# Output copies of a block at the end of one slot, and x split on VectorE in one place

## The chip, the cores and the metric

The kernel runs on one core of a Trainium2 chip. The metric is the device time of one execution in microseconds, as the median of several runs; less is better. Five engines work beside each other: TensorE (PE; its weight loads are shown apart as PEld), VectorE (DVE), ScalarE (ACT), GpSimd (POOL) and SyncE (SP), whose queue issues the kernel's DMAs. Each engine runs its own instructions strictly in the order of the program, and waits for the others through semaphores.

## The reference

Attention inside chunks of 64 tokens, then two feed-forward layers, all in fp32 from the reader's point of view:

```python
# q, k, v: 8 batches, 8 heads, 576 tokens, 64 wide; chunks of 64
scores = scale * q_c @ k_c.T ; scores -= max ; attn = exp(scores)
attn = attn / (attn.sum(-1) + 1e-9) ; x = (attn @ v_c) laid out as (4608 tokens, 512)
h = x @ w_in                                   # 512 -> 2048
g = where(h > 0, h, exp(min(h, 0)) - 1)        # ELU
y = g @ w_out                                  # 2048 -> 512
out = (sigmoid(y @ w_gate) * (y @ w_val)) @ w_out2   # 512 -> 1536 -> 512
```

## The kernel before

**Numbers.** Every product of a feed-forward layer is made of three fp32r matmuls: each operand is split into a rounded high part and a low part (raw minus high), and high x high, low x high and high x low are summed in PSUM (PASSES). To split a tile takes a cast on one engine and a subtraction on another (split, L94 to L96). The weights come as 64-bit numbers and are converted on the chip: a tile of raw bits is loaded on SP's queue (load, L118) and goes through ScalarE steps (magnitude L124, low L128, high) and five VectorE steps (clamp, shift, sign, add L146, rest L155). add also issues the load of the raw tile that is *ahead* places further on, which takes over the buffer that add has just read. bg(n) puts n such steps into the program.

**Blocks and slots.** The 4608 tokens are 9 blocks of 512 (j = 0 to 8). Phase A goes through each block in 16 slots (f = 0 to 15, s = 16 j + f). slot(s) (L461) writes out by hand what each engine does in a slot; nothing is reordered later. In a slot PE does, in this order: one attention product (scores of a pair of chunks in an even slot, values in an odd one, four matmuls on the PSUM tile banks), the first layer of slot s (layer_1: 12 matmuls into h, three for each of the four x tiles kk = 0 to 3), and the second layer of slot s - 2 (layer_2: 12 matmuls that add into four PSUM banks y0 to y3, one bank for each e). The y banks fill over a block: the last addition for block j - 1 is in slot f = 1 of block j, and in slot f = 2 the first layer_2 of block j overwrites them. Between the two lie the four copies of y_out (L449: e even on ScalarE, L456; e odd on VectorE, L458), each followed by a DMA to ymid on SP (L459).

**The elementwise work of a slot.** ScalarE and VectorE turn h into g: elu_exp (L405) and elu_rest (L408) on ScalarE, elu_sum (L411) on VectorE one slot later, then elu_split (cast on ScalarE, L90; subtraction on VectorE, L96). The attention of a pair runs over four slots: first_parts copies half of banks to s1 on ScalarE (L297), softmax_max (L310 to L312), softmax_exp (L315), softmax_sum, and blocks_out (a VectorE transpose to dt, L339, and eight small DMAs to tt, L346); two slots later transposes_split makes pt from tt (L92 and L96 on VectorE, two casts on ScalarE, L357), which the values product (L379) of the slot after needs as weights. In odd slots VectorE also splits the next pair's operands (L248, L256 to L258) and writes the pair's result into xr (L395).

**The x tiles.** xr0 to xr3 hold the attention result of the next block, xs0 to xs3 its split halves; there is one buffer of each, so xs of the next block can be written only when layer_1 of slot f = 15 has read the old one, and layer_1 of slot f = 0 needs it 16 matmuls later. Before, split_x (L182) is called at four places: x0 in slot 15 ahead of the second half of layer_1 (subtraction on GpSimd), x1 behind elu_split (VectorE), x2 behind elu_rest (GpSimd), x3 at the start of slot f = 0 (VectorE). The cast is always ScalarE's.

**Buffers.** The pool e gives out 3 buffers of 2 KB a partition, in turn to the elu tiles, the y copies, and in phase B to the sigmoid and output tiles. s1, dt and tt have 2 buffers each. Phase B (L685) runs the last block of phase A and then the second network, in slots of 36 matmuls (pg, pv at L189, o at L730), while it converts 36 weight tiles with 4 raw buffers.

Of the kernel before, what the change touches and what calls it, by code (L numbers as in the profile page):

```python
# [8 lines left out]
F32 = mybir.dt.float32  # L9
# [8 lines left out]
CH = 64  # L18
# [5 lines left out]
NB = NT // TB  # L24
NG = NT // 128 * (H // 2)
GPB = NG // NB
KC = DM // 128
# [25 lines left out]
def kernel(  # L53
# [23 lines left out]
    nc = tc.nc  # L77
# [3 lines left out]
    w_p = ctx.enter_context(tc.tile_pool(name="w", bufs=2 * F1))  # L81
    x_p = ctx.enter_context(tc.tile_pool(name="x", bufs=1))
    g_p = ctx.enter_context(tc.tile_pool(name="g", bufs=2))
    e_p = ctx.enter_context(tc.tile_pool(name="e", bufs=3))
    ps_y = ctx.enter_context(tc.tile_pool(name="ps_y", bufs=1, space=bass.MemoryType.PSUM))
    ps_h = ctx.enter_context(tc.tile_pool(name="ps_h", bufs=2, space=bass.MemoryType.PSUM))

# [94 lines left out]
    def split_x(key, kk, lo_eng):  # L182
        x = xs[key, kk] = x_p.tile([128, 2, TB], F32R, tag=f"xs{kk}", name=f"xs{kk}")
        split(xr.pop((key, kk)), x[:, 0], x[:, 1], nc.scalar, lo_eng)
# [18 lines left out]
    def phase_a():  # L203
        with (
# [7 lines left out]
            raws, vals, qv, kz, st = {}, {}, {}, {}, {}  # L212
# [79 lines left out]

            def first_parts(P, what):

                t = st[P, what + "1"] = s_p[0].tile([128, 4, CH], F32, tag="s1", name="s1", bufs=2)
                for a, p in enumerate(halves):
                    nc.scalar.copy(out=t[p], in_=parts_of(st[P, what], p, a)[0])  # L297

# [36 lines left out]

            def blocks_out(P):

                d = s_p[0].tile([128, 2, 4, 32], F32, tag="dt", name="dt", bufs=2)
                nc.vector.transpose(  # L339
                    out=d.rearrange("p b n q -> p n b q"),  # L340
                    in_=st.pop((P, "p")).rearrange("p n (b k) -> p n b k", b=2),
                )
                t = st[P, "tt"] = s_p[0].tile([64, 4, 128], F32, tag="tt", name="tt", bufs=2)
                for b in range(2):
                    for w in range(4):
                        nc.sync.dma_start(  # L346
                            out=t[32 * b:32 * b + 32, w],
                            in_=d[32 * w:32 * w + 32, b].rearrange("p n q -> p (n q)"),
                        )
# [99 lines left out]
            def y_out(j, es=range(KC)):  # L449
                for e in es:  # L450
                    if j == NB - 2:
                        y = xr_tile("y", e)
                    else:
                        y = e_p.tile([128, TB], F32, tag="e", name="y")
                    if e % 2 == 0:
                        nc.scalar.copy(out=y, in_=y_t.pop((j, e)))  # L456
                    else:
                        nc.vector.tensor_copy(out=y, in_=y_t.pop((j, e)))  # L458
                    nc.sync.dma_start(out=ymid[j][:, e], in_=y)  # L459

            def slot(s, steps=0):  # L461


                j, f = divmod(s, F1)
                q = [steps // 4 + (i < steps % 4) for i in range(4)]
                last = f == F1 - 1
                nxt = j + 1 if j + 1 < NB else ("b", 0)
                even = s % 2 == 0
                P, T, V, N = s // 2 + 1, (s + 1) // 2, (s - 1) // 2, (s + 3) // 2

                def is_pair(n, least=0):
                    return least <= n < NP

                if even:
                    if is_pair(P + 1, P32):
                        load_raw(P + 1)
                    if is_pair(P):
                        scores(P)
                    if is_pair(P, P32):
                        first_parts(P, "s")  # L480
                else:
                    if is_pair(V):
                        values(V)
                    if is_pair(V, P32):
                        first_parts(V, "v")
                    elif is_pair(V):
                        values_out(V)
                if f == 0 and j > 0:
                    split_x(j, KC - 1, nc.vector)
                if s >= F1:  # L490
                    elu_sum(s - 1)
                if even and is_pair(P):
                    softmax_max(P)
                if even and is_pair(P, P32):
                    softmax_exp(P)
                if even and is_pair(P - 1, P32):
                    transposes_split(P - 1)
                if even and is_pair(P, P32):
                    softmax_sum(P)
                    blocks_out(P)  # L500
                if not even:
                    if is_pair(N, P32):
                        split_k(N)
                    if is_pair(V, P32):
                        values_out(V)
                    if is_pair(N, P32):
                        split_qkv(N)
                bg(q[0])
                if 0 < s < F1:
                    elu_sum(s - 1)  # L510
                if s >= EARLY:
                    layer_1(s, 2)
                if f == 2 and j > 0:
                    y_out(j - 1, (2, 3))
                if s == F1 - 1:

                    layer_1(s, 3)
                    transposes(T)
                    transposes_out(T)
                if last:  # L520
                    split_x(nxt, 0, nc.gpsimd)
                bg(q[1])
                layer_1(s)
                if s > 0:
                    elu_split(s - 1)
                if even and 0 <= P < P32:
                    softmax_exp(P)
                if last:
                    split_x(nxt, 1, nc.vector)
                now = not even and 0 <= T < P32 and s >= F1  # L530
                if now:
                    transposes(T)
                elu_exp(s)
                if now:
                    transposes_out(T)
                if even and PB <= P < P32:
                    softmax_sum(P)
                bg(q[2])
                if 0 < s <= F1:
                    elu_low(s - 1)  # L540
                elu_rest(s)
                if last:
                    split_x(nxt, 2, nc.gpsimd)
                bg(q[3])
                if even and is_pair(P) and P < PB:
                    softmax_sum(P)
                if s >= 2:
                    layer_2(s - 2)
                if not even and is_pair(T) and s < F1 - 1:
                    transposes(T)  # L550
                    transposes_out(T)
                if f == 1 and j > 0:
                    y_out(j - 1, (0, 1))

            def first_block(load_w):

# [128 lines left out]
    def phase_b(slot, layer_2, elu_sum, elu_split, y_out):  # L685
        with (
# [2 lines left out]
            tc.tile_pool(name="ps_b", bufs=2, space=bass.MemoryType.PSUM) as ps_b,  # L689
        ):  # L690
            tiles = [(k, w_src[k[0]][k[1]], w_p if n < 2 * F1 else w2_p) for n, k in enumerate(w2)]
            load_w = convert(tiles, conv_p, 4, 4)
            for n in range(4):
                load_w(n)
            for s in range((NB - 1) * F1, NB * F1):
                slot(s, A8_STEPS if s < NB * F1 - 1 else 0)
# [157 lines left out]
```

## Time and profile before

| what | value |
|---|---|
| median of 3 runs | 1809.66 us (1807.86 to 1810.4) |
| profiled execution, device time | 1808.78 us |
| its span, first to last instruction | 1807.0 us |
| PE busy | 1776.1 us, 98% |
| VectorE busy | 1044.9 us, 58% |
| ScalarE busy | 757.1 us, 42% |
| GpSimd busy | 44.2 us, 2% |

The profile page gives the busy time of each engine over the whole span, the same in 40 slices, the chain of work that ended last, and groups of instructions by line. The answers of the trace that are used below are the list of waits (who waited for whom, in total), and timelines: every instruction in order of time, with equal neighbours merged (xN), and in brackets the idle time of the engine before it and what ended it. A PE row's length is modelled and overlaps the next row; the distance between the starts of two PE rows is what counts.

### The profile page before, as it was taken

What the parts mean: (1) busy time and instruction counts of PE and PEld (TensorE: products, weight loads), DVE (VectorE), ACT (ScalarE), POOL (GpSimd) and SP (SyncE); (2) the same over time, 40 slices, a digit from 0 to 9 for tenths busy, and PEclk for the clock granted to TensorE, in tenths of its full rate; (3) what the DMA queues carried; (4) which work ended last, traced back from release to release, by engine and by line L of the source; (5) the groups of instructions that cost most, each with busy time, mean ns of one, the idle gap of its engine ahead of it and who ended that gap; (6) DMA issues with size and microseconds to landing.
All of it is one profiled execution on the core that took longest, in us unless ns stands there. A gap on an engine that the chain in (4) does not pass through costs nothing.

```text
span 1807.0 us, 21535 instructions
## 1 busy us (share of the span) xinstructions
PE 1776.1 (98%) x8068; PEld 1471.1 (81%) x8068; DVE 1044.9 (58%) x1980; ACT 757.1 (42%) x1411; POOL 44.2 (2%) x50
## 2 busy tenths in 40 slices
PE   7999999999999999999999999999999999999999
PEld 6887878788888878788888888888888888888887
DVE  7997888888888888887767423222222222222322
ACT  7775666767666766767654201010110101010101
POOL 1000000000000000000000000000000000000000
PEclk9999999999999999999999999999999999999999
DMA  6652121121212122215343101000010101010000
GB/s 231 200 169 77 57 80 59 58 69 53 74 57 82 48 79 59 69 47 166 117 128 106 47 1 47 1 24 24 9 38 0 47 0 48 1 47 1 24 1 24
DMA packets 61593, 111.52 MB, mean 62 GB/s; under 512 B 11056, under 2 KB 30000, under 8 KB 61488
## 3 DMA queue, kind: packets, MB, share of 16 engines
q1 hardware_dynamic: 61488, 110.14, 19.3%
q8 instruction: 63, 1.03, 0.2%
q14 instruction: 42, 0.34, 0.1%
HBM read 84.15 MB, written 18.87 MB: 57 GB/s over the span
## 4 chain that ended last, share of the span: by engine, by line
PE 83%; DVE 9%; ACT 5%; issue 1%; DMA 1%; SPq 0%; POOL 0%; DVEq 0%
PE o L730 16%; PE pv L189 16%; PE pg L189 16%; PE y L441 16%; PE h L189 15%; PE banks L379 1%; PE banks L280 1%; ACT pt L357 1%; DVE t L140 1%; DVE elu L411 1%; DVE s L310 1%; DVE w L155 1%; DVE xs L96 1%; DVE qv L258 1%; DVE t L146 1%
## 5 line engine op out<-in xcount | busy, mean ns | idle before, releaser
L189 PE MATMUL h<-xs,w 128*128 128x512 f32 x1728 | 426.3, 394 | 5.7 <-DVE xs L96 3.9
L441 PE MATMUL y<-g,w 128*128 128x512 f32 x1728 | 419.5, 391 | 8.3 <-ACT y L456 7.6
L719 DVE TENSOR_TENSOR sg<-pv,sg 128x512 f32<-128x512 f32 x108 | 74.6, 691 | 548.6 <-PE pv L189 545.6
L441 PEld LDWEIGHTS y<-g,w 128*128 128x128 f32 x1728 | 323.2, 188 | 80.2 <-ACT y L456 10.1
L189 PEld LDWEIGHTS h<-xs,w 128*128 128x128 f32 x1728 | 317.1, 189 | 69.0 <-DVE xs L96 6.4
L714 ACT ACTIVATE sg<-pg 128x512 f32<-128x512 f32 x108 | 64.5, 597 | 676.9 <-PE pg L189 676.6
L189 PE MATMUL pv<-xs,w 128*128 128x512 f32 x1296 | 311.3, 389 | 0.0
L189 PE MATMUL pg<-xs,w 128*128 128x512 f32 x1296 | 311.3, 389 | 0.0
L730 PE MATMUL o<-w,g 128*128 128x512 f32 x1296 | 311.1, 389 | 0.0
L189 PEld LDWEIGHTS pv<-xs,w 128*128 128x128 f32 x1296 | 243.2, 188 | 50.5
L189 PEld LDWEIGHTS pg<-xs,w 128*128 128x128 f32 x1296 | 243.2, 188 | 50.5
L730 PEld LDWEIGHTS o<-w,g 128*128 128x128 f32 x1296 | 243.2, 188 | 50.5
L411 DVE SCALAR_TENSOR_TENSOR elu<-h,elu 128x512 f32<-128x512 f32 x144 | 99.4, 690 | 65.5 <-ACT elu L408 64.2
L405 ACT ACTIVATE elu<-h 128x512 f32<-128x512 f32 x144 | 86.0, 597 | 53.6 <-PE h L189 25.6
L297 ACT COPY s<-banks 64x256 f32<-64x256 f32 x216 | 78.2, 362 | 67.5 <-PE banks L280 64.3
L90 ACT CAST g<-elu 128x512 fp32r<-128x512 f32 x144 | 89.3, 620 | 23.0 <-DVE elu L411 18.5
L408 ACT ACTIVATE elu<-elu 128x512 f32<-128x512 f32 x144 | 90.9, 631 | 3.8
L96 DVE TENSOR_TENSOR g<-elu,g 128x512 fp32r<-128x512 f32 x128 | 87.9, 686 | 6.3 <-ACT g L90 4.6
L96 DVE TENSOR_TENSOR g<-sg,g 128x512 fp32r<-128x512 f32 x108 | 74.9, 694 | 3.7
L96 POOL TENSOR_TENSOR xs<-xr,xs 128x512 fp32r<-128x512 f32 x26 | 36.8, 1417 | 1631.1 <-ACT xs L90 1631.1
L315 ACT ACTIVATE e<-s 128x256 f32<-128x256 f32 x64 | 26.8, 418 | 111.2 <-DVE s L312 110.7
L357 ACT CAST pt<-pt 64x512 fp32r<-64x512 f32 x108 | 66.8, 619 | 4.5 <-DVE pt L92 2.2
(86 smaller groups left out, 1299.2 us busy)
## 6 DMA issues: line engine op xcount, KB each, us to landing
raw<-in_qkv SPq DMA_DIRECT2D x54, 512.0 KB, 3.7
wraw<-in_w_out SPq DMA_DIRECT2D x28, 512.0 KB, 3.5
xr<-ymid SPq DMA_DIRECT2D x36, 256.0 KB, 3.6
wraw<-in_w_in SPq DMA_DIRECT2D x16, 512.0 KB, 3.7
ymid<-y SPq DMA_DIRECT2D x32, 256.0 KB, 3.1
out<-o SPq DMA_DIRECT2D x32, 256.0 KB, 2.0
tt<-dt SPq DMA_DIRECT2D x432, 16.0 KB, 1.8
wraw<-in_w_gate SPq DMA_DIRECT2D x12, 512.0 KB, 3.6
```

Of the source, the lines that this page charges most:

```text
L90: nc.scalar.copy(out=out, in_=raw)
L96: lo_eng.tensor_sub(out=lo, in0=raw, in1=hi)
L189: nc.tensor.matmul(out=ps, lhsT=w[:, zw, kk * 128:(kk + 1) * 128], rhs=xs[key, kk][:, zx], start=(kk == 0 and n == 0), stop=(kk == KC - 1 ...
L297: nc.scalar.copy(out=t[p], in_=parts_of(st[P, what], p, a)[0])
L357: nc.scalar.copy(out=t[h1, z], in_=t[h0, z])
L405: nc.scalar.activation(out=e_t[s], in_=h_t[s], func=ACTF.Exp)
L408: nc.scalar.activation(out=e_t[s], in_=e_t[s], func=ACTF.Relu, scale=-1.0, bias=1.0)
L411: nc.vector.scalar_tensor_tensor(out=e_t[s], in0=h_t.pop(s), scalar=0.0, in1=e_t[s], op0=ALU.max, op1=ALU.subtract,)
L441: nc.tensor.matmul(out=y_t[j, e], lhsT=w[:, zw, e * 128:(e + 1) * 128], rhs=g[:, zx], start=(f == 0 and n == 0), stop=(f == F1 - 1 and n = ...
L714: nc.scalar.activation(out=sg, in_=pg, func=ACTF.Sigmoid)
L719: nc.vector.tensor_tensor(out=sg, in0=pv, in1=sg, op=ALU.mult)
L730: nc.tensor.matmul(out=o_t[t], lhsT=g[:, zx, t * 128:(t + 1) * 128], rhs=w[:, zw], start=(f == 0 and n == 0), stop=(f == F2 - 1 and n == 2),)
```

## The change

- All four output copies of block j - 1 are called at the end of slot f = 1 of block j. Before, y0 and y1 stood there, and y2 and y3 in slot f = 2 behind the first half of layer_1.
- The four split_x of a block are called in a row in slot f = 15, right behind layer_1 and ahead of elu_split, all with the subtraction on VectorE. For the switch to phase B only three are made there; the fourth stays where it was.
- The pool e has 5 buffers instead of 3. s1, dt and tt have 1 instead of 2, and phase B has 3 raw weight buffers instead of 4.

```diff
-    e_p = ctx.enter_context(tc.tile_pool(name="e", bufs=3))
+    e_p = ctx.enter_context(tc.tile_pool(name="e", bufs=5))
...
-                t = st[P, what + "1"] = s_p[0].tile([128, 4, CH], F32, tag="s1", name="s1", bufs=2)
+                t = st[P, what + "1"] = s_p[0].tile([128, 4, CH], F32, tag="s1", name="s1")
...
-                d = s_p[0].tile([128, 2, 4, 32], F32, tag="dt", name="dt", bufs=2)
+                d = s_p[0].tile([128, 2, 4, 32], F32, tag="dt", name="dt")
...
-                t = st[P, "tt"] = s_p[0].tile([64, 4, 128], F32, tag="tt", name="tt", bufs=2)
+                t = st[P, "tt"] = s_p[0].tile([64, 4, 128], F32, tag="tt", name="tt")
...
-                if f == 0 and j > 0:
-                    split_x(j, KC - 1, nc.vector)
...
-                if f == 2 and j > 0:
-                    y_out(j - 1, (2, 3))
...
-                if last:
-                    split_x(nxt, 0, nc.gpsimd)
                 bg(q[1])
                 layer_1(s)
+                if last:
+                    for kk in range(KC if j + 1 < NB else KC - 1):
+                        split_x(nxt, kk, nc.vector)
                 if s > 0:
                     elu_split(s - 1)
...
-                if last:
-                    split_x(nxt, 1, nc.vector)
...
-                if last:
-                    split_x(nxt, 2, nc.gpsimd)
...
                 if f == 1 and j > 0:
-                    y_out(j - 1, (0, 1))
+                    y_out(j - 1)
...
-            load_w = convert(tiles, conv_p, 4, 4)
-            for n in range(4):
+            load_w = convert(tiles, conv_p, 3, 4)
+            for n in range(3):
                 load_w(n)
```

**VectorE, from slot 15 of block 2 to slot 0 of block 3.** The rows run from the split of q (qv) to the first softmax rows (s) of the next slot; xs_N is a split x tile, made from xr_N; the fp32 subtraction g is elu_split's. Before:

```order
L258 TENSOR_TENSOR qv<-raw,qv 64x2x256
L96 TENSOR_TENSOR g<-elu,g 128x512
L96 TENSOR_TENSOR xs_3403<-xr_2783,xs_3403 128x512
L96 TENSOR_TENSOR xs_3433<-xr_3257,xs_3433 128x512
L411 SCALAR_TENSOR_TENSOR elu<-h,elu 128x512
L310 TENSOR_TENSOR s<-banks,s_3430 64x256 x2
```

And after the change:

```order
L258 TENSOR_TENSOR qv<-raw,qv 64x2x256
L96 TENSOR_TENSOR xs_3397<-xr_2530,xs_3397 128x512
L96 TENSOR_TENSOR xs_3400<-xr_2783,xs_3400 128x512
L96 TENSOR_TENSOR xs_3403<-xr_3020,xs_3403 128x512
L96 TENSOR_TENSOR xs_3406<-xr_3257,xs_3406 128x512
L96 TENSOR_TENSOR g<-elu,g 128x512
L411 SCALAR_TENSOR_TENSOR elu<-h,elu 128x512
L310 TENSOR_TENSOR s<-banks,s_3433 64x256 x2
```

Two subtractions have come over from GpSimd, and all four now stand ahead of the subtraction of g.

**ScalarE, at the same place**, from the casts of q to the first_parts copy (s_N, the name of s1) of slot 0. Before:

```order
L255 CAST qv<-raw 64x2x256
L90 CAST xs_3391<-xr_2530 128x512
L90 CAST g<-elu 128x512
L90 CAST xs_3403<-xr_2783 128x512
L405 ACTIVATE elu<-h 128x512
L408 ACTIVATE elu<-elu 128x512
L90 CAST xs_3409<-xr_3020 128x512
L297 COPY s_3430<-banks 64x256 x2
L90 CAST xs_3433<-xr_3257 128x512
```

And after the change:

```order
L255 CAST qv<-raw 64x2x256
L90 CAST xs_3397<-xr_2530 128x512
L90 CAST xs_3400<-xr_2783 128x512
L90 CAST xs_3403<-xr_3020 128x512
L90 CAST xs_3406<-xr_3257 128x512
L90 CAST g<-elu 128x512
L405 ACTIVATE elu<-h 128x512
L408 ACTIVATE elu<-elu 128x512
L297 COPY s_3433<-banks 64x256 x2
```

The same casts in another order: the last x cast stands ahead of the copy to s1 instead of behind it, and g's cast and the two activations come two or three casts later.

**ScalarE, from slot 1 to slot 2 of block 3**, around the output copies (y from the PSUM banks y_N). Before:

```order
L456 COPY y<-y_2639 128x512
L297 COPY s_3558<-banks 64x256 x2
L315 ACTIVATE e_93<-s 128x4x64
L357 COPY pt<-pt 64x512 x2
L456 COPY y<-y_2641 128x512
L90 CAST g<-elu 128x512
```

And after the change:

```order
L456 COPY y<-y_2639 128x512
L456 COPY y<-y_2641 128x512
L297 COPY s_3564<-banks 64x256 x2
L315 ACTIVATE e_93<-s 128x4x64
L357 COPY pt<-pt 64x512 x2
L90 CAST g<-elu 128x512
```

The copy of y2 has moved from behind the softmax chain of slot 2 to the end of slot 1. On VectorE the copy of y3 has moved in the same way, from behind the transpose to dt of slot 2 to a place right behind the copy of y1, ahead of elu_sum.

## Rows read from the trace of the kernel before

**Rows 1.** The page's head and its busy times, shares and instructions.

```profile
span 1807.0 us, 21535 instructions
PE 1776.1 (98%) x8068; PEld 1471.1 (81%) x8068; DVE 1044.9 (58%) x1980; ACT 757.1 (42%) x1411; POOL 44.2 (2%) x50
```

**Rows 2.** Waits of PE: total us, times, longest; all rows on layers' products.

```profile
PE y L441 <- ACT y L456: 7.6, 6, 1.3
...
PE h L189 <- DVE xs L96: 3.9, 6, 0.7
...
PE y L441 <- DVE y L458: 0.7, 1, 0.7
PE h L189 <- POOL xs L96: 0.6, 1, 0.6
```

**Rows 3.** Timeline (start us, us, engine, line), slots 15 to 1, blocks 2 to 3.

```profile
334.98 0.62 ACT L90 CAST xs<-xr 128x512 fp32r<-128x512 f32 x1
...
335.31 2.89 PE L441 MATMUL y<-g,w 128*128 128x512 f32 x12
...
335.68 1.78 POOL L96 TENSOR_TENSOR xs<-xr,xs 128x512 fp32r<-128x512 f32 x1 [94.13 <-ACT xs L90]
...
336.33 1.67 DVE L258 TENSOR_TENSOR qv<-raw,qv 64x512 fp32r<-64x512 f32 x1
...
338.03 0.69 DVE L96 TENSOR_TENSOR g<-elu,g 128x512 fp32r<-128x512 f32 x1
...
338.52 1.31 PE L189 MATMUL h<-xs,w 128*128 128x512 f32 x5
...
338.64 2.39 DVE L96 TENSOR_TENSOR xs<-xr,xs 128x512 fp32r<-128x512 f32 x2
...
340.49 1.88 PE L189 MATMUL h<-xs,w 128*128 128x512 f32 x7 [0.65 <-DVE xs L96]
341.06 0.69 DVE L411 SCALAR_TENSOR_TENSOR elu<-h,elu 128x512 f32<-128x512 f32 x1
...
345.21 0.54 PEld L379 LDWEIGHTS banks<-pt,qv 128*128 128x128 f32 x4 [0.55 <-ACT pt L357]
345.22 0.75 PE L379 MATMUL banks<-pt,qv 128*128 128x256 f32 x4
```

**Rows 4.** Timeline from the end of slot 1 to slot 3 of block 3.

```profile
350.38 0.69 DVE L258 TENSOR_TENSOR qv<-raw,qv 64x512 fp32r<-64x512 f32 x1
...
351.76 2.90 PE L189 MATMUL h<-xs,w 128*128 128x512 f32 x12
351.90 0.69 DVE L458 COPY y<-y 128x512 f32<-128x512 f32 x1
...
354.50 1.52 PE L441 MATMUL y<-g,w 128*128 128x512 f32 x6
...
355.34 1.26 ACT L357 CAST pt<-pt 64x512 fp32r<-64x512 f32 x2
...
356.62 0.58 ACT L456 COPY y<-y 128x512 f32<-128x512 f32 x1
...
357.26 1.91 PE L441 MATMUL y<-g,w 128*128 128x512 f32 x6 [1.24 <-ACT y L456]
...
359.01 0.64 PE L379 MATMUL banks<-pt,qv 128*128 128x256 f32 x4
```

**Rows 5.** Raw weight tiles, 920 to 1010 us: time from issue to landing.

```profile
DMA to landing us min/median/max: 3.3/3.5/3.7
```

**Rows 6.** Timeline of a phase B slot with conversion.

```profile
937.83 0.33 SPq L118 DMA_DIRECT2D wraw<-in_w_gate  x1
...
939.37 0.66 ACT L124 ACTIVATE t<-wraw 128x512 f32<-128x512 f32 x1
...
941.63 0.69 DVE L96 TENSOR_TENSOR g<-sg,g 128x512 fp32r<-128x512 f32 x1
...
948.34 2.88 PE L730 MATMUL o<-w,g 128*128 128x512 f32 x12
```

## Prediction

> **What bounds the kernel now.** I read the page's head first: PE is busy for 1776.1 of 1807.0 us [rows 1]. A change that takes no matmul away can only win back what PE waits for, so the list of PE's waits comes next. Four of its rows belong to what is edited: for the ScalarE output copy 7.6 us in 6 waits, for the VectorE copy 0.7, for the split of x by VectorE 3.9 in 6, by GpSimd 0.6 [rows 2]. That is 12.8 us, and it comes in equal portions at block boundaries: six alike, and the first boundary with the two single waits. The other two of the nine switches have no such row. Last I read the timeline of one boundary, to see who is late behind each wait.
>
> An undisturbed layer sets the scale: twelve matmuls from 351.76 to 354.50, 2.74 us [rows 4].
>
> *x.* layer_1 of slot 0 starts at 338.52 and the values product of slot 1 at 345.22, 6.70 us for 24 matmuls that need 5.48; 1.22 is lost. The reader should see two waits in it: the row at 340.49 waits 0.65 for a VectorE subtraction of x, and the weight load at 345.21 waits 0.55 for pt, the end of the softmax chain on VectorE and ScalarE [rows 3]. So behind the x wait VectorE itself is late. Why it is late stands just above: L258 takes 1.67 us, though the same instruction takes 0.69 in slot 1 [rows 3, 4], and two x subtractions take 2.39 together where a subtraction of the same size takes 0.69 [rows 3]. Both lie beside or right behind GpSimd's subtractions of x.
>
> *y.* layer_2 of slot 2 starts at 354.50 and the values product of slot 3 at 359.01: 4.51 instead of 2.74, 1.77 lost. The third y bank waits 1.24 us for a ScalarE copy that starts only at 356.62, when the softmax chain ahead of it in ScalarE's queue has let go (pt's casts end at 355.34 + 1.26 = 356.60) [rows 4].
>
> **Part by part.** *The x splits.* Removed: two GpSimd subtractions a boundary, and with them what they hold up on VectorE: 1.67 - 0.69 = 0.98 and 2.39 - 1.38 = 1.01. Added: two more subtractions on VectorE at 0.69. Consecutive VectorE rows stand 0.03 apart (336.33 + 1.67 = 338.00, next row 338.03), so I take 0.72 a piece. From L258 at 336.33 six such instructions (L258, x0 to x3, g) bring elu_sum to 340.65, where it starts at 341.06 now [rows 3]: 0.41 earlier. Behind elu_sum the order of the chain to pt is unchanged, so pt comes 0.41 earlier and the values product starts at 344.81. Are the x tiles ready? ScalarE is free at 334.98 and casts four tiles at 0.62, to about 337.5; the old xs tiles are read by 335.5, since layer_2 starts at 335.31 [rows 3]. The subtractions end at 337.8, 338.5, 339.2 and 339.9, and PE, starting at 338.52 with 0.69 a tile, wants them at 338.5, 339.2, 339.9 and 340.6. So no x wait, with 0.7 to spare. But PE then reaches the values product at 338.52 + 5.48 = 344.00 and waits 0.8 there for pt: of the 1.22 lost, only **0.41** comes back. The g cast, now behind four x casts, ends near 338.2; its subtraction comes at 339.9 and PE wants it at 341.3.
>
> By what is shown, then, VectorE gets back 1.99 us; a mechanism that gives back more is the second rival.
>
> *The output copies.* Nothing is removed; y2 and y3 move ahead of slot 2's softmax chain. ScalarE's y2 follows y0, long before 354. On VectorE y1 and y3 at 0.69 [rows 4] end near 352.2 and 352.9 (with the shift of 0.41), and the banks are overwritten from 354.09 on: the 1.24 wait goes. The price is what queues behind y3 on VectorE: elu_sum and the whole chain to pt, later by 0.72. With the shift pt ends at 356.60 - 0.41 + 0.72 = 356.91. PE arrives at 354.09 + 2.74 = 356.83. So this wait all but closes too; I put the values product at 356.97 instead of 359.01. A boundary gives **2.04**, 1.63 of it here.
>
> *Six boundaries:* 12.2. *The first:* the two single waits are 0.6 and 0.7; a wait's row understates the loss, as the one of 0.65 shows (five matmuls from 338.52 end at 339.66, PE goes on at 340.49: 0.83), so 1.66. Its pairs still have the older form, whose values product needs no pt, and nothing else is late: 1.6. *The last two switches:* attention has ended, nothing waits, 0.
>
> *The buffers.* e: ScalarE's waits for a free tile go; none is in PE's list. If an elu tile falls on a y buffer, its DMA is issued by 353 and lands by 357 (3.7 for a tile of twice the size [rows 5]), when elu_exp is still behind pt's casts and g's cast. s1: the copy that would overwrite it reads banks after a product that itself waited for the VectorE reads of banks, the same instructions that read s1: no new wait. tt and dt: the reads of the old tt stand ahead of the transpose on VectorE, and they waited for the eight DMAs that read the old dt: no new wait. SP: the DMAs of y2 and y3 pass ahead of the next pair's load and its eight tt DMAs; they hold the queue until y3's copy at 352.9, and that load is wanted only in slot 3, after 357. GpSimd has nothing else in phase A. The raw weight buffers are the third rival; 0 here.
>
> Sum: 12.2 + 1.6 = 13.8. The profiled execution took 1808.78 (span 1807.0), so 1795.0; the median shown is 0.9 above that execution: **1796**, 1793 to 1799 with 0.5 more or less a boundary.
>
> **Rivals.** *First, VectorE remains the bound.* If L258 is long for a reason other than GpSimd, elu_sum starts at 336.33 + 1.70 + 5 x 0.72 = 341.63, 0.57 later than now. x then costs 0.57, pt of slot 3 comes at 356.60 + 0.57 + 0.72 = 357.89, and a boundary gives about 1.1: 6.4 + 1.6 = 8 us, 1801. For it: no VectorE row there has idle time ahead of it [rows 3], and two more instructions come. Against it: L258 is 0.69 in slot 1 [rows 4].
>
> *Second, GpSimd costs VectorE more than the two stretched rows show.* If each GpSimd subtraction holds VectorE for its whole 1.78 [rows 3], 3.56 come back instead of 1.99, 1.6 more than counted, which covers both the 0.8 and what is left at y: 1.22 + 1.77 = 2.99 a boundary, 17.9 + 1.6 = 19.5, 1790. Against it: 0.69 of L258 is its own time, so its stretch was 0.98 and no more. The Trainium skill, page "SBUF — State Buffer", section "Who interferes with whom", states this rule: a VectorE instruction with two SBUF inputs and a GpSimd instruction that reads SBUF exclude each other, and the loser blocks fully. The trace agrees that they collide; it shows 0.98 and 1.01 rather than whole instructions.
>
> *Third, and slower: three raw weight buffers starve the conversion.* With 3, a raw tile's load is issued where the next tile's is now. In phase B such a load goes out at 937.83 and the ScalarE step that would need it starts at 939.37 [rows 6], 1.54 later; landing takes 3.5 [rows 5]. ScalarE would stand for 1.96, with the sigmoid and the casts of w queued behind it, and VectorE waits for those. By the code 15 slots of 6 steps do half of the 36 tiles in block 8, so some 15 tiles load like this: 29 us of holds. They reach PE only beyond the slack of g: it is ready at 941.63 + 0.69 = 942.32 and used at 948.34 [rows 6], 6.0 later. If nothing is caught up between slots, 29.4 - 6.0 = 23.4 is lost, net 9.6 slower: 1818. Against it: a slot of 36 matmuls (8.2) does 9 steps, 1.8 tiles, so three buffers come round every 13.7; a round takes landing 3.5, the ScalarE step 0.66, seven VectorE steps and two times three of gating at 0.72 at most, 13.5. It fits, so holds don't add up; it decides from a landing of about 4 to 5 us, and the longest is 3.7. The Trainium skill's opening page, "Trainium Kernel Development and Optimization", section "Best Practices", says to double-buffer so that DMA overlaps compute, which speaks against every buffer cut here; if it bit, it would be at this place.
>
> *Fourth, the change doesn't do what it says:* an elu tile on a y buffer or another queue restores the waits, within 3.6 us of now. The order of instructions speaks against it.
>
> **How the numbers follow.** The forecast 0.57, the first rival 0.16, the second 0.12, the third 0.09, the fourth 0.06. The first three are faster by over 0.2% (3.6 us, about what a measurement of this kernel can tell from no change): 0.85; within 0.2% 0.06; slower 0.09. Forecast and first rival hold 0.73, too little, so the range reaches to the second as well: 1790 to 1802.
>
> **What would show it.** Right: PE's waits for y and for x gone from its list at all boundaries; a wait for pt of about 0.8 left in slot 1 and next to none in slot 3; L258 at 0.69 in slot 15; some 2 us less from one boundary to the next. L258 still long: first rival. No pt wait: second. ScalarE waiting for raw tiles some 2 us each after 930 is expected; PE waiting for g there is the third. Any PE wait for a DMA would prove the buffer reasoning wrong.

## The result, and the profile after

The changed kernel took 1791.84 us (median of 3, 1790.42 to 1791.86) where the kernel before took 1809.66: 0.9901 of its time, with a 95% interval of 0.9878 to 0.9923. It is 17.8 us faster. The forecast was 13.6 faster, 1796, with 1790 to 1802 as the range. The profiled execution took 1790.42. Three kernels had one execution each that took far longer, in a slow state of the chip (2978 us for the x part alone, 2214 for the old engines at the new place, 5721 for the kernel before), and their medians below are those of the other executions.

The page's head of the kernel after, to be read against [rows 1]:

```profile
span 1788.5 us, 21632 instructions
...
PE 1770.7 (99%) x8068; PEld 1472.7 (82%) x8068; DVE 1040.2 (58%) x1998; ACT 759.0 (42%) x1411; POOL 17.7 (1%) x32
```

VectorE makes 18 subtractions more (1980 to 1998) and is yet busy for less, 1040.2 instead of 1044.9. The four waits of [rows 2] are gone from PE's list (total us, times, longest). This row is all that is left at the boundaries; the others in the list belong to the kernel's start:

```profile
PE banks L379 <- ACT pt L357: 1.4, 6, 0.2
```

The timeline of VectorE, ScalarE and PE from slot 15 of block 2 to slot 1 of block 3, to be read against [rows 3]:

```profile
331.30 0.69 DVE L258 TENSOR_TENSOR qv<-raw,qv 64x512 fp32r<-64x512 f32 x1
...
332.02 2.50 DVE L96 TENSOR_TENSOR xs<-xr,xs 128x512 fp32r<-128x512 f32 x4
...
333.46 2.90 PE L189 MATMUL h<-xs,w 128*128 128x512 f32 x12
...
334.44 0.68 DVE L96 TENSOR_TENSOR g<-elu,g 128x512 fp32r<-128x512 f32 x1
335.15 0.69 DVE L411 SCALAR_TENSOR_TENSOR elu<-h,elu 128x512 f32<-128x512 f32 x1
...
339.31 0.75 PE L379 MATMUL banks<-pt,qv 128*128 128x256 f32 x4 [0.23 <-ACT pt L357]
```

L258 is back at 0.69. layer_1's twelve matmuls run through without a wait, and from their start to the values product it is 5.85 (333.46 to 339.31), where [rows 3] show 6.70. The four subtractions of x take 2.50 together, and the row behind them starts 2.42 after the first: 0.605 apiece. Next, slot 1 to slot 3, the place of [rows 4]:

```profile
344.96 1.05 ACT L456 COPY y<-y 128x512 f32<-128x512 f32 x2
345.20 0.69 DVE L96 TENSOR_TENSOR g<-elu,g 128x512 fp32r<-128x512 f32 x1
...
345.93 1.29 DVE L458 COPY y<-y 128x512 f32<-128x512 f32 x2
...
347.13 0.68 DVE L411 SCALAR_TENSOR_TENSOR elu<-h,elu 128x512 f32<-128x512 f32 x1
...
348.60 2.88 PE L441 MATMUL y<-g,w 128*128 128x512 f32 x12
...
349.97 1.26 ACT L357 CAST pt<-pt 64x512 fp32r<-64x512 f32 x2
...
351.32 0.71 PE L379 MATMUL banks<-pt,qv 128*128 128x256 f32 x4
```

All copies are done before layer_2 of slot 2 starts, and from its start to the values product it is 2.72 instead of 4.51: 1.79 won. A phase B slot, the place of [rows 6]:

```profile
928.83 0.67 ACT L124 ACTIVATE t<-wraw 128x512 f32<-128x512 f32 x1 [2.34 <-DMA wraw<-in_w_gate]
...
930.34 2.88 PE L723 MATMUL o<-w,g 128*128 128x512 f32 x12
```

This o product started at 948.34 before: 18.00 earlier now. The same distance holds through the rest of phase B, so the gain comes from phase A, but for the 0.5 us by which the span gets shorter behind the last matmul. ScalarE now does stand for raw tiles; its rows of the waits from 911 to 990 us:

```profile
ACT t L124 <- DMA wraw<-in_w_gate: 8.8, 4, 2.5
...
ACT t L124 <- DMA wraw<-in_w_val: 6.9, 4, 2.4
...
ACT t L124 <- DMA wraw<-in_w_out: 5.4, 4, 2.3
```

That is 21.1 us in 12 waits, and no PE row answers to them.

### The profile page after: what moved, and what is told of

It is laid out like the page before. It is cut to its first block, busy times and chain, and to the rows that moved or that the text cites. A ratio compares the mean times of both kernels' runs of the same rounds, so it can differ in the third digit from the quotient of the medians.

```text
span 1788.5 us, 21632 instructions
## 1 busy us (share of the span) xinstructions
PE 1770.7 (99%) x8068; PEld 1472.7 (82%) x8068; DVE 1040.2 (58%) x1998; ACT 759.0 (42%) x1411; POOL 17.7 (1%) x32
## 4 chain that ended last, share of the span: by engine, by line
PE 92%; ACT 4%; DVE 3%; DMA 0%; issue 0%; SPq 0%; DVEq 0%
PE y L441 19%; PE h L189 19%; PE o L723 16%; PE pv L189 16%; PE pg L189 16%; PE banks L379 1%; PE banks L280 1%; ACT pt L357 1%; DVE xs L96 1%; DVE s L310 1%; DMA qkv<-in_qkv 0%; ACT s L297 0%; PE bank L266 0%; ACT xs L90 0%; ACT xr L647 0%
## 5 line engine op out<-in xcount | busy, mean ns | idle before, releaser
L411 DVE SCALAR_TENSOR_TENSOR elu<-h,elu 128x512 f32<-128x512 f32 x144 | 99.4, 690 | 47.8 <-ACT elu L408 46.4
L96 DVE TENSOR_TENSOR xs<-xr,xs 128x512 fp32r<-128x512 f32 x60 | 43.0, 761 | 46.1 <-ACT xs L90 45.9
```

Source lines behind the costliest of these rows:

```text
L96: lo_eng.tensor_sub(out=lo, in0=raw, in1=hi)
L411: nc.vector.scalar_tensor_tensor(out=e_t[s], in0=h_t.pop(s), scalar=0.0, in1=e_t[s], op0=ALU.max, op1=ALU.subtract,)
```

## The experiments

Below, "y part" is the output copies with their buffers, "x part" the splits of x. Ratios are to the kernel before, with 95% intervals.

**The x part alone**, in the kernel before:

```diff
-                if f == 0 and j > 0:
-                    split_x(j, KC - 1, nc.vector)
...
-                if last:
-                    split_x(nxt, 0, nc.gpsimd)
                 bg(q[1])
                 layer_1(s)
+                if last:
+                    for kk in range(KC if j + 1 < NB else KC - 1):
+                        split_x(nxt, kk, nc.vector)
...
-                if last:
-                    split_x(nxt, 1, nc.vector)
...
-                if last:
-                    split_x(nxt, 2, nc.gpsimd)
```

> The kernel before with one part alone: the four x splits in a row in slot 15, all on VectorE; output copies and buffers as before. Theory (VectorE is what PE waits for at a boundary, and the splits hand it time back): each of the six boundaries gives 0.85 us (in the changed kernel the first layer of slot 0 starts at 333.46 and the values product of slot 1 at 339.31, 5.85 instead of 6.70), the first 0.8, so 5.9 us: 1804. The loss at the output copies stays, since the ScalarE copy of y2 still follows the softmax chain. Rival (the five buffers of e carry part of the gain, since ScalarE's and VectorE's waits for a free e tile go): well under 3 us here, 1807 or more.

Measured: 1802.12, ratio 0.9961 (0.9947 to 0.9976), 6.9 us below the 1809.05 of before. Its waits are read from one further execution.

> The kernel before with the x splits alone once more, for its profile: 1802 to 1804; no wait of PE for x; the wait for pt in slot 1 about 0.4 instead of the 0.3 lost before; the waits for the output copies as before, about 1.3 in each of six boundaries.

Measured: 1802.82. PE's waits:

```profile
PE y L441 <- ACT y L456: 7.6, 6, 1.3
...
PE banks L379 <- ACT pt L357: 1.7, 6, 0.6
```

The copies' wait is the old one, the wait for x is gone, and a wait for pt has come up behind it.

**The y part alone**: the changed kernel with the four splits at their old places and on their old engines.

```diff
+                if f == 0 and j > 0:
+                    split_x(j, KC - 1, nc.vector)
...
+                if last:
+                    split_x(nxt, 0, nc.gpsimd)
                 bg(q[1])
                 layer_1(s)
-                if last:
-                    for kk in range(KC if j + 1 < NB else KC - 1):
-                        split_x(nxt, kk, nc.vector)
...
+                if last:
+                    split_x(nxt, 1, nc.vector)
...
+                if last:
+                    split_x(nxt, 2, nc.gpsimd)
```

> The changed kernel with the x splits put back to their four old places (two on GpSimd); the output copies in slot 1 and all buffers as changed. Theory: the waits of PE for the output copies go, and y3 ahead of the softmax chain delays pt by about 0.7, which leaves a wait of 0.1: 1.65 a boundary, 0.9 at the first, 10.8 us: 1799. The x wait of 0.65 and the pt wait behind it stay. Rival (the two parts need each other: without time handed back, y3 on VectorE pushes pt past PE): 6 us or less, 1804 or more.

Measured: 1797.51, ratio 0.9935 (0.9919 to 0.9951), 11.5 us below before. PE's list keeps the x wait of before and has lost both rows of the copies:

```profile
PE h L189 <- DVE xs L96: 3.9, 6, 0.7
```

6.9 and 11.5 make 18.4: the parts add up to what the whole gives (17.8), so neither needs the other. The traces say the same without the kernel's start and end. From the middle of block 0 to phase B, PE's matmuls gain 5.9 us on the kernel before with the x part, 11.0 with the y part and 17.6 with both.

**The buffers alone**: the y part without the move of the copies.

```diff
+                if f == 2 and j > 0:
+                    y_out(j - 1, (2, 3))
...
                 if f == 1 and j > 0:
-                    y_out(j - 1)
+                    y_out(j - 1, (0, 1))
```

> The kernel before with the buffers of the change alone (e 5, s1, dt and tt 1, raw weights 3); all splits and copies at their old places. Theory: PE never waits for a buffer, so nothing moves: 1809.7 within 1.5, with the same waits of PE; ScalarE's waits for an e tile go and its waits for raw tiles in phase B come. Rival (five e tiles let ScalarE run ahead and bring pt or y2 forward): 2 to 5 us faster. Other rival (single s1, dt, tt cost a wait): slower by 2 us or more.

Measured: 1808.86, ratio 0.9998 (0.9989 to 1.0008). The counts of buffers by themselves, more in e and fewer elsewhere, give and cost nothing.

**The new order with three buffers in e**: the changed kernel with

```diff
-    e_p = ctx.enter_context(tc.tile_pool(name="e", bufs=5))
+    e_p = ctx.enter_context(tc.tile_pool(name="e", bufs=3))
```

> The changed kernel with 3 buffers in the pool e again. Theory (the five buffers are needed for the order, not by themselves): the copy of y2 on ScalarE and of y3 on VectorE must wait until the DMAs of y0 and y1 have landed, some 3.5 us after their copies; the softmax chain of slot 2 stands behind both, pt comes about 3.5 later and PE waits that long in slot 3 at six boundaries and about 1 at the first: 21 to 25 us more than the changed kernel, 1813 to 1817, slower than the kernel before. Rival (buffers don't matter, as at the old order): 1791.8.

Measured: 1813.22, ratio 1.0022 (1.0012 to 1.0032): slower than before, as expected. A row of PE's waits and the timeline behind slot 1 show why:

```profile
PE banks L379 <- ACT pt L357: 18.2, 12, 3.0
```

```profile
353.37 0.59 ACT L456 COPY y<-y 128x512 f32<-128x512 f32 x1 [4.29 <-DMA ymid<-y]
...
354.01 0.69 DVE L458 COPY y<-y 128x512 f32<-128x512 f32 x1 [3.76 <-DMA ymid<-y]
...
358.73 0.75 PE L379 MATMUL banks<-pt,qv 128*128 128x256 f32 x4 [3.00 <-ACT pt L357]
```

y2 and y3 need tiles that the DMAs of earlier y copies still read. Both engines stand until these have landed, with the softmax chain queued behind, and PE waits 3.00 for pt. Of the 23 us above the changed kernel measured beside it (1790.09, below), these waits make some 17 (18.2 instead of 1.3); a part of the rest goes with the clock, as the last section shows. So the five buffers are no gain of their own, yet the new order needs them.

**The old engines at the new place**:

```diff
-                        split_x(nxt, kk, nc.vector)
+                        split_x(nxt, kk, nc.gpsimd if kk % 2 == 0 else nc.vector)
```

> The changed kernel with two of the four x subtractions (x0, x2) on GpSimd again, at their new place. Theory (GpSimd's subtraction holds up VectorE's): VectorE has two subtractions less (2 x 0.60) but loses about 1.0 beside each GpSimd one, L258 or its neighbours are stretched again, elu_sum comes 0.8 later and the wait for pt in slot 1 grows from 0.4 to 1.2: about 4.8 us more than the changed kernel's 1791.8, 1796.6. Rival (GpSimd costs VectorE nothing, the gain was only that x comes in time): VectorE is 1.2 earlier, the pt wait in slot 1 is gone, 1789.5.

Measured: 1795.11, ratio 0.9923 (0.9905 to 0.9941). VectorE has two subtractions fewer, and yet the kernel is 3.3 us slower than the 1791.84 of the changed kernel, and 5.0 slower than its second measurement below. A row of PE's waits, then VectorE and GpSimd in the timeline:

```profile
PE banks L379 <- ACT pt L357: 4.3, 6, 0.7
```

```profile
331.82 1.78 POOL L96 TENSOR_TENSOR xs<-xr,xs 128x512 fp32r<-128x512 f32 x1 [93.28 <-ACT xs L90]
...
332.47 1.67 DVE L258 TENSOR_TENSOR qv<-raw,qv 64x512 fp32r<-64x512 f32 x1
...
333.55 1.74 POOL L96 TENSOR_TENSOR xs<-xr,xs 128x512 fp32r<-128x512 f32 x1
...
334.17 1.67 DVE L96 TENSOR_TENSOR xs<-xr,xs 128x512 fp32r<-128x512 f32 x1
```

L258 is 1.67 again, 0.98 longer than alone, and so is the first subtraction of x behind it. PE's wait for pt grows from 1.4 to 4.3. This is the reverse of the edit in the change, so the stretch comes from GpSimd's subtractions.

**The new engine at the old places**: the y part alone, with VectorE for GpSimd.

```diff
-                    split_x(nxt, 0, nc.gpsimd)
+                    split_x(nxt, 0, nc.vector)
...
-                    split_x(nxt, 2, nc.gpsimd)
+                    split_x(nxt, 2, nc.vector)
```

> The changed kernel with the four x splits at their old places in the program, but all four subtractions on VectorE: only the engine of x0 and x2 is changed, not the place. Theory (the place counts too, through ScalarE: at its old place the cast of x3 stands behind the copy to s1, which waits for PE's scores): the subtraction of x3 can start only some 0.6 later than in the changed kernel, elu_sum and pt come 0.55 later, PE waits about 0.3 for x3: 3 to 4 us more than the changed kernel, 1794. Rival (only GpSimd counted, the place is nothing): 1791 within 1.

Measured: 1795.56, ratio 0.9925 (0.9908 to 0.9941). Without either step it is 1797.51 (the y part alone): the place alone and the engine alone win some 2 us each, both together some 6. (From the middle of block 0 to phase B, the traces have 11.0 with neither, 12.8 with either one, 17.6 with both.) L258 is 0.69 here, at the old place, so its stretch went with the engine. But x3 is late, since its cast stands behind the copy to s1, which waits for PE. PE's row for pt, then VectorE and ScalarE:

```profile
PE banks L379 <- ACT pt L357: 5.5, 6, 1.2
```

```profile
332.77 0.69 DVE L258 TENSOR_TENSOR qv<-raw,qv 64x512 fp32r<-64x512 f32 x1
...
335.13 0.75 ACT L297 COPY s<-banks 64x256 f32<-64x256 f32 x2 [0.25 <-PE banks L280]
...
335.88 0.62 ACT L90 CAST xs<-xr 128x512 fp32r<-128x512 f32 x1
...
336.54 0.69 DVE L96 TENSOR_TENSOR xs<-xr,xs 128x512 fp32r<-128x512 f32 x1 [0.56 <-ACT xs L90]
```

The expected wait of PE for x3 itself did not come. The loss lies in the row for pt, 5.5 us instead of 1.4.

**The changed kernel once more**, as the measure for the runs around it. The three buffers above and the next two ran beside it; the two raw buffers and the turned halves ran later, beside the kernel before alone.

> The changed kernel itself once more, as the mark for the runs beside it: 1791.8 within 1.5.

Measured: 1790.09 (1789.53 to 1791.53), ratio 0.9897 (0.9882 to 0.9912).

**One more subtraction** behind those of x; its result is not used.

```diff
+                if last and j + 1 < NB:
+                    x = xs[nxt, 0]
+                    spare = e_p.tile([128, TB], F32, tag="e", name="spare")
+                    nc.vector.tensor_sub(out=spare, in0=x[:, 0], in1=x[:, 1])
                 if s > 0:
```

> The changed kernel with one subtraction more on VectorE, of the same size, behind the four of a boundary; its result is not used. Theory (VectorE is the bound from slot 15 to the values product of slot 1): each of the six boundaries costs the full spacing of one such row, 0.60, and the wait of PE for pt in slot 1 grows by that: 3.6 us, 1795.4. Rival (VectorE has room there): within 1 us of the changed kernel.

Measured: 1793.30, ratio 0.9916 (0.9901 to 0.9931), 3.2 us above the run beside it. A row of PE's waits, then two of VectorE's timeline:

```profile
PE banks L379 <- ACT pt L357: 5.3, 6, 1.2
```

```profile
333.80 0.69 DVE L524 TENSOR_TENSOR spare<-xs 128x512 f32<-128x512 f32 x1
334.40 0.69 DVE L96 TENSOR_TENSOR g<-elu,g 128x512 fp32r<-128x512 f32 x1
```

One instruction with a row of 0.69 moves the next by 0.60, and PE's wait for pt grows by (5.3 - 1.4) / 6 = 0.65 a boundary. VectorE sets the end at x, and the step from start to start is what an instruction costs there, not its row with a gap added.

**The chain to pt ahead of elu_sum** in slots 0 and 2, which takes one instruction of VectorE off the path to pt:

```diff
-                if s >= F1:
+                late_sum = even and f in (0, 2) and is_pair(P, P32) and s >= F1
+                if s >= F1 and not late_sum:
                     elu_sum(s - 1)
...
                     transposes_split(P - 1)
+                if late_sum:
+                    elu_sum(s - 1)
```

> The changed kernel with elu_sum of the slot before moved in slots f = 0 and f = 2 from ahead of the softmax rows on VectorE to behind the making of pt; the work is the same. Theory (what PE still waits for at a boundary is VectorE's chain to pt): pt comes 0.6 earlier, which is more than the 0.4 lost in slot 1 and the 0.1 in slot 3, so six boundaries give 0.45 each, 2.7 us: 1789. Rival (pt waits for ScalarE or for the tt DMAs, not for VectorE's order): no change, 1791.8. Other rival (elu_sum later holds up g and the h banks): slower.

Measured: 1787.79 (1786.52 to 1788.15), ratio 0.9882 (0.9867 to 0.9897), the best of all that ran, 2.3 below the changed kernel beside it. No row for pt is left in PE's list, and its rows are all of the kernel's start now. The longest:

```profile
PE ps_s L585 <- DMA qkv<-in_qkv: 7.0, 4, 3.5
```

**Two raw weight buffers** in phase B:

```diff
-            load_w = convert(tiles, conv_p, 3, 4)
-            for n in range(3):
+            load_w = convert(tiles, conv_p, 2, 4)
+            for n in range(2):
```

> The changed kernel with 2 raw weight buffers in phase B instead of 3. Theory (the third rival of the prediction is a real mechanism that 3 buffers just escape): a load is issued one VectorE step ahead of the ScalarE step that needs it, ScalarE stands for 3.5 and VectorE for about 2.5 us a tile; a tile then takes 2.9 + 2.5 and its share of the gating or of the elu work, 6.4 against the 4.5 at which the program deals them out; 18 tiles in block 8 and 18 in phase B lag by some 2 each, less 6 of slack in either: 40 to 60 us, 1830 to 1850. Rival (ScalarE and VectorE have enough room in phase B for any wait): within 5 us of the changed kernel.

Measured in a single execution: 1867.42, 77 us above the changed kernel. The direction was foreseen, the size (40 to 60) was not. PE's two longest rows, and the longest of ScalarE's three for raw tiles:

```profile
PE o L723 <- DVE g L92: 22.5, 7, 4.3
PE y L441 <- ACT g L90: 18.8, 12, 3.2
```

```profile
ACT t L124 <- DMA wraw<-in_w_out: 53.8, 12, 6.0
```

PE now waits for g, as the prediction's third rival had it. The two rows make 41.3 of the 77; a part of the rest goes with a lower granted clock (0.91 from 800 to 900 us, 0.95 from 900 to 1000), and how much is not shown.

**The halves of values_out in the other order**, in the changed kernel:

```diff
-                for a, p in enumerate(halves):
+                for a, p in reversed(list(enumerate(halves))):
```

> The changed kernel, but values_out (L395) adds its two halves of the partitions in the other order, the upper half first and the lower one last. It asks why neighbours on VectorE stand 0.72 apart in one place and 0.60 in another. In the changed kernel L411 starts 0.71 behind a subtraction of g (334.44, 335.15) and the copy of y1 0.73 behind g (345.20, 345.93), but the subtractions of x stand 0.60 apart, and so does L411 behind the copies of y. Theory: an instruction waits for the end of the one ahead when its input or output begins at another partition (0 or 64) than in the last instruction that read or wrote the same memory. Ahead of L411 and y1 the last reader of PSUM was the upper half of L395; ahead of the faster ones it was one from partition 0. With the lower half last, L411 and y1 start 0.60 to 0.61 behind g; the first L395 row starts at the end of the cast of k (L248), no longer 0.085 before it, and L256 some 0.08 before the end of L395, not 0.03 behind it. PE's waits for pt in slot 1 (1.4 us in 6) fall by 0.11 each, to 0.7, and the time by 0.7 to 1.5, to 1789 to 1791. The Trainium skill states such a rule: page 'VectorE: DVE Perf Modes', section 'Two Vector instructions with no wait between them'. Rival: L411 and y1 start late because they read PSUM behind an instruction that read only SBUF, whatever stood before. Then they stay 0.71 to 0.73 behind g, and the time at 1790 to 1792.

Measured: 1789.44 (1788.11 to 1790.89), ratio 0.9891 (0.9874 to 0.9907), which can't be told from 1790.09; the rows can. VectorE's timeline:

```profile
328.84 0.42 DVE L248 CAST kz<-raw 128x512 fp32r<-128x512 f32 x1
329.29 0.86 DVE L395 TENSOR_TENSOR xr<-banks,s 64x256 f32<-64x256 f32 x2
330.07 0.67 DVE L256 TENSOR_TENSOR kz<-raw,kz 128x512 fp32r<-128x512 f32 x1
...
334.63 0.69 DVE L96 TENSOR_TENSOR g<-elu,g 128x512 fp32r<-128x512 f32 x1
335.23 0.68 DVE L411 SCALAR_TENSOR_TENSOR elu<-h,elu 128x512 f32<-128x512 f32 x1
```

L411 starts 0.60 behind g instead of 0.71, the first half of L395 begins 0.03 behind the end of the cast of k instead of 0.085 ahead of it, and L256 begins 0.08 before the end of L395 instead of 0.03 behind it. All three came out as the first theory had them, and so did the copy of y1, 0.61 behind g. The rival (PSUM behind SBUF) falls. PE's row for pt (1.4 in 6) is gone from the list, where a half of it was to stay. From the middle of block 0 to phase B the trace is 18.9 ahead of the kernel before, where the changed kernel is 17.6 ahead: 1.3 us, within the 0.7 to 1.5 expected.

## Why the prediction was right, and by how much it missed

**What bounds, and where the gain lies: right.** Of the 18.5 us by which the span is shorter, 17.6 came from the block boundaries, phase B gave 0, and the two parts of the change add up. The number is a weaker hit. 1791.84 lies below the forecast's own 1793 to 1799, and in the stated range only because that was stretched to the second rival's 1790, whose sum does not hold (below). That part is luck.

**The x splits: the mechanism right, one size wrong.** L258 went from 1.67 to 0.69, no x wait came, and PE came to wait for pt instead, each as written. The step that was off is "Consecutive VectorE rows stand 0.03 apart, so I take 0.72 a piece". From L258 to L411 the sum had six of these, 4.32; measured are 335.15 - 331.30 = 3.85. Two of the six (from L258 to x0, from g to L411) are 0.72; four (x0 to x3, then g) are 0.605, 0.115 less each, together 0.46. So elu_sum came 0.88 and not 0.41 earlier, x gave 6.70 - 5.85 = 0.85, and the wait for pt put at 0.8 came out at 0.23. The price was already to be read in [rows 3]: the subtraction of g at 338.03 is followed at 338.64, 0.61 later. The pair from L258 to g was taken in its place, and that is the slower kind.

**Why two neighbours differ.** Over the whole trace of the changed kernel, neighbours on VectorE that wait for no other engine fall into kinds. In the most common one the next row starts before the end of the one ahead, by 0.05 to 0.09, mostly 0.083. In the second it starts 0.031 behind that end. These are the pairs in which an input or output begins at another partition (0 or 64) than the last one in the same memory: from L256 to L257, to L258 and to the row after it; from the second half of L395 to L256; and from g to L411 or to the copy of y1, which read PSUM where L395's upper half was the last reader. (The two halves of L395 and of L310 also change partition, and stand 0.014 apart.) A row that uses the result of the row ahead starts 0.034 behind its end. Turning the halves moved four pairs from one kind to the other as this says (L248 to L395, L395 to L256, g to L411, g to y1), so the rule is shown for them; for the pairs at L257 and L258 it is only in agreement.

The Trainium skill states it, page "VectorE: DVE Perf Modes", section "Two Vector instructions with no wait between them": as a model, an instruction is held until the earlier ones have finished where the start quadrant (of 32 partitions) of an input differs from that of the last read of the same memory, or that of its output from the last write. The traces agree, with the numbers above.

**The output copies: right.** 1.63 was forecast, 1.79 came. pt ends 349.97 + 1.26 - 348.60 = 2.63 after the start of layer_2, forecast 2.82 (356.91 - 354.09). Of the 0.19 between them, 0.12 is the same term again, since y3 stands 0.60 and not 0.72 behind y1; the other 0.07 is that y1 stood 0.80 behind g before and stands 0.73 now. A boundary gave 0.85 + 1.79 = 2.64, not 2.04.

**The sum.** Six boundaries gave about 2.6 each instead of 2.04, 3.4 us more in all; the first 1.9 instead of 1.6. The rest of the 18.5 by which the span is shorter is 0.4 at the kernel's start and 0.5 at its end. Both are small and the start differs between executions of one kernel: in a second one of the changed kernel the first block ended 1.3 earlier than before, not 0.4.

**The buffers: right in the cost, wrong in a "no new wait".** They cost 0 alone (0.9998), and ScalarE's waits for a free e tile (15.2 us in 6 before) are gone as forecast. But with one tt and one dt, SP's queue now stands for the landing of earlier tt DMAs, in a row that the kernel before does not have:

```profile
SPq L346 <- DMA tt<-dt: 25.5, 48, 1.3
```

None of it reaches PE: VectorE waits for these DMAs once, for 0.8, before and after.

**First rival (VectorE remains the bound): out.** L258 was long because of GpSimd alone; with GpSimd back it is 1.67, and without it 0.69, at the new place and at the old one.

**Second rival (GpSimd gives back 3.56 us): out, though its number, 1790, was the nearest.** What came back is 0.98 at L258 and 1.10 at the pair of x, which took 2.39 and alone takes 0.605 + 0.69 = 1.29 (the prediction had 1.01, from rows set end to end). Two more subtractions at 0.605 cost 1.21 of these 2.08. That leaves 0.87, and elu_sum came 0.88 earlier: the sum closes with nothing more from GpSimd, and what was missing came from the spacing. A forecast judged by its time alone would have picked the wrong cause here.

The Trainium skill's rule on this, page "SBUF — State Buffer", section "Who interferes with whom", is that the two exclude each other and the loser blocks fully. The prediction took the 0.98 as less than that, but the traces agree with the rule; what the second rival had wrong is the price. Three more rows of the kernel before, the last two from the switch into block 1:

```profile
335.61 0.69 DVE L257 TENSOR_TENSOR qv<-raw,qv 64x512 fp32r<-64x512 f32 x1
```

```profile
139.82 0.69 DVE L411 SCALAR_TENSOR_TENSOR elu<-h,elu 128x512 f32<-128x512 f32 x1
140.05 1.29 POOL L96 TENSOR_TENSOR xs<-xr,xs 128x512 fp32r<-128x512 f32 x1 [108.09 <-ACT xs L90]
```

Where VectorE comes second, its row ends 0.55 behind GpSimd's: L258 at 338.00 behind 337.46 [rows 3], and with the old engines at the new place 334.14 behind 333.60 and 335.84 behind 335.29. Where GpSimd comes second, its row ends 1.16 behind VectorE's (337.46 behind L257's 336.30). So the two run one after the other. L258 loses only 0.98 because GpSimd's row of 1.78 was under way when L258 came, and had itself stood for L257: beside elu_sum, which has only one input in SBUF, both rows keep their lengths, 0.69 and 1.29.

**Third rival (raw buffers): the mechanism real, not reached.** With three, ScalarE waits 21.1 us in the stretch above and PE nothing; with two, PE waits for g and 77 us are lost. The bound of a round, 13.5 of 13.7, put the limit at the right side of three. (Its 1818 leaves out the 0.9 that the forecast adds, and would be 1819.)

**Fourth rival: out** with five buffers, and with three it is what happened: the waits come back, and larger ones.

## What to carry to other kernels

Price an instruction added to a busy engine by the step from one start to the next in a row of like neighbours, and look for the kind of neighbour it will have (same start partition or another, dependent or not), for that one term, 0.72 instead of 0.605, made most of the miss here. A step handed from one engine to another may give back more than its own time when the two engines exclude each other: here two subtractions cost VectorE 2.08 us on GpSimd and 1.21 on VectorE itself. When copies are drawn together into one place, count the buffers that are in flight at once: the same order won 18 us with five and lost 4 with three. Where a moved wait has closed, the next one is already in the trace; here it was pt, and putting its chain ahead of an elementwise step that nobody waits for gave 2 us more. That step and the turned halves were not tried together.

## What the runs showed of the hardware

Behind some of PE's waits of 2.5 to 3.0 us the granted clock fell. The kernel with three buffers in e has six such waits for pt; here are its windows around one of them (us; busy us of PE, PEld, DVE, ACT, POOL; granted clock; DMA share; GB/s), and the timeline of PE there:

```profile
545.00:556.00 11.00, 8.23 (x38) 6.49 (x37) 7.68 (x16) 5.02 (x10) 0.00 (x0) 0.98 0.48 150
556.00:562.50 6.50, 6.40 (x17) 5.20 (x18) 5.78 (x11) 4.41 (x10) 0.00 (x0) 0.52 0.08 23
562.50:575.00 12.50, 12.50 (x60) 10.46 (x59) 8.52 (x19) 8.40 (x16) 0.00 (x0) 1.00 0.14 50
```

```profile
556.10 1.22 PE L379 MATMUL banks<-pt,qv 128*128 128x256 f32 x4 [2.88 <-ACT pt L357]
...
557.12 5.31 PE L189 MATMUL h<-xs,w 128*128 128x512 f32 x12
...
562.24 1.12 PE L441 MATMUL y<-g,w 128*128 128x512 f32 x4
```

For 6.5 us the granted clock is 0.52, the lower of the two levels (1.2 of 2.4 GHz), and twelve matmuls take 562.24 - 557.12 = 5.12 instead of 2.74. So this wait cost 2.88 and then nearly as much again. It happened behind two of the six, of 2.88 (556.10) and 2.48 (657.30), and not behind the other four, of 2.58, 3.00, 2.52 and 3.00 (259.20, 358.73, 457.42 and 758.03). So the length of the wait alone does not decide it; what does, these runs don't show.
